# K scaled by GpSimd ahead of its transposes, and weight sums spread over two more phases, in a fused attention and gate kernel

## The chip, the cores and the metric

The kernel runs on one core of a Trainium2 chip. The metric is the device time of one execution, in microseconds (us). Every execution also has a mean granted TensorE clock: 1.0 is full speed, and TensorE runs at half speed for some microseconds after certain gaps. The mean is taken over the whole span, so half clock after the last matmul counts in it although it costs nothing.

## The reference, cut to what matters

Two branches read the same layer-normed `x` (2048 rows, 640 columns). One is attention with 32 heads of 192 columns over the last 512 rows of a key and value cache; the other is a gated feed-forward net (1536 hidden columns), whose output gates the first.

```python
q = (xn @ wq).reshape(B, Sq, 32, 192).transpose(0, 2, 1, 3)
scores = einsum("bhqd,bhkd->bhqk", q, k_last_512) * (192 ** -0.5)
s = (softmax(scores) @ v_last_512).transpose(...).reshape(B, Sq, 32 * 192) @ wo
h = sigmoid(xn @ w_gate) * (xn @ w_up)
g = silu(h @ w_down)
return x + s * g
```

## The kernel before

It first computes the gates (four stages of 512 rows, the last one ending at about 166 us) and stores them in device memory. Then it goes through 16 attention runs: 8 groups of 4 heads, each for two halves of the rows. Run r computes its scores (with the query projection of run r+1 between them) and then its weighted sums of V (with the output product of run r-1 between them). Only run 0 has its projection, "the first projection", by itself. In the views, `hT` is the hidden tile of the gate part, `gB` the finished gates, `qp` a copy of a projected query part and `qT` the finished query tile; a bank is a piece of the memory into which TensorE writes its results (`ps_all`), and HI is the second group of matmuls of the first projection, which needs VectorE's first query sum. Comments in the code cuts are mine, and `...` marks what is left out.

The query weights are scaled by a power of two (`w_up`), split into halves and added and subtracted in float16 (`scale_w` on ScalarE, `sum_w` on VectorE). Each group of heads has five such parts. The inverse of that scale is made up for in the Exp, which reads it from a one-column tile:

```python
def set_scale2(mx_row):
    ...
    nc.vector.tensor_scalar(w_down, mx, 1.0 / 4096, None, op0=ALU.mult)
    nc.vector.reciprocal(w_up, w_down)
    nc.vector.tensor_scalar(w_down, w_down, scale_qk, None, op0=ALU.mult)

def scale_w(g, c):                                   # ScalarE: 1.57 + 2 x 0.52 us
    raw = raw_t[g, c][:]
    nc.scalar.activation(raw.bitcast(F16), raw, AF.Copy, scale=w_up)
    for k, r in enumerate((LO, HI)):
        nc.scalar.activation(sums_w(g, c, r, 0), part_w(g, c, r, k, 0), AF.Copy)

def sum_w(g, c):                                     # VectorE: 4 x 0.36 us, ScalarE: 0.52 us
    ...
    tt(TB, part_w(g, c, a, 1, 1), part_w(g, c, a, 0, 1), ALU.subtract)     # two inputs in SBUF
    ...

def stage_s(r, i, pp, c, k):                         # scores: 6 matmuls and an Exp
    ...
    nc.scalar.activation(E_t[r, i, pp][:, c, :, :], ps, AF.Exp, scale=w_down)

def stage_pv(r, i, pp, h):                           # 16 matmuls, then VectorE
    if h == 0:
        ost_t[0] = (late["ost"] if r == last else ost_pool).tile(..., name="o_st")
    ...                                              # ost_pool has two buffers
    if h == 1:
        nc.sync.dma_start_transpose(oT[:], o_st[:]...)
```

The memory of the gate part is given to the pools of the attention part, in this order: `acc_pool`, `wo_pool`, `qT_pool`, `e_pool`, `ost_pool`, ... The first query tiles (`qT`) come to lie where the gate tiles (`gB_sb`) were, so whoever writes them waits for the last gate store.

The softmax here doesn't subtract the row's maximum and nothing guards it: scores larger than these inputs give would overflow.

Of the kernel before, what the change touches and what calls it, by code (L numbers as in the profile page):

```python
# [17 lines left out]
def kernel(  # L18
# [13 lines left out]
    nc = tc.nc  # L32
# [98 lines left out]
    def load_k(key):  # L131
# [6 lines left out]
            )  # L138
        k_of[key] = k_sb

    def turn_k(key):
        kT = kt_pool.tile([P, KC * PC, P], BF16, name="kT")
        nc.sync.dma_start_transpose(kT[:], k_of[key][:].rearrange("p n i e -> p (n i e)"))
        kT_t[key] = kT
# [43 lines left out]
    def set_scale2(mx_row):  # L188
        nc.vector.tensor_reduce(mx, mx_row[:], axis=mybir.AxisListType.X, op=ALU.max)
        nc.vector.tensor_scalar(mx, mx, 1e-30, None, op0=ALU.max)  # L190
        bits = mx.bitcast(I32)
        nc.vector.tensor_single_scalar(bits, bits, 0x7F800000, op=ALU.bitwise_and)
        nc.vector.tensor_scalar(w_down, mx, 1.0 / 4096, None, op0=ALU.mult)
        nc.vector.reciprocal(w_up, w_down)
        nc.vector.tensor_scalar(w_down, w_down, scale_qk, None, op0=ALU.mult)

    def load_raw(g, c, eng):
        raw = raw_pool.tile([P, 2, GC], BF16, name="raw")
# [31 lines left out]
    with ExitStack() as bctx:  # L230
# [185 lines left out]
        for s in range(NST):  # L416
# [4 lines left out]
            for f in range(NF):  # L421
# [26 lines left out]
                if s == 1 and f < NSB:  # L448
                    scan_load(NSB + f, nc.gpsimd)
                elif s == 2 and f < NPC - 2 * NSB:  # L450
                    scan_load(2 * NSB + f, nc.gpsimd)
                elif s == 2 and f < 5:
                    load_raw(0, f - 2, nc.gpsimd)
                elif s == 2 and f == 6:
                    set_scale(wmax, mx_row)
                elif s == 2 and f == NF - 1:
                    set_scale2(mx_row)
                elif s == 3:
                    if f == 0:
                        weight_tiles(0)  # L460
                    for c in {0: (0,), 2: (1,), 5: (2,), 7: (3,), 10: (4,)}.get(f, ()):
                        scale_w(0, c)
                    for c in {1: (0,), 3: (1,), 6: (2,), 8: (3,), 11: (4,)}.get(f, ()):
                        sum_w(0, c)
                        load_raw((c + 3) // NCD, (c + 3) % NCD, nc.gpsimd)
                    if f in (2, 6):
                        turn_k((0, f // 4))
                        load_k(divmod(f // 4 + 1, G))
            if s + 2 < NST:
                load_x4(s + 2)  # L470
            for q in range(TQ):
# [13 lines left out]
                    scan_fold(wmax, folds_q[s, q])  # L485
                if s == 3 and q in (1, 2):
                    sum_x(pi, 3 + q, sw)
                t = s * TQ + q
                nc.gpsimd.dma_start(gB_d[t * P:(t + 1) * P, :], gB_sb[:])
            if s == 0:  # L490
# [24 lines left out]
    wo_t = {}  # L515

    def load_wo(g):
        pool, eng = (late["wo"], nc.sync) if g == NG - 1 else (wo_pool, nc.scalar)
        wo_g = pool.tile([P, G * PC, D], BF16, name="wo_g")
        eng.dma_start(wo_g[:], wo_r[:, g * G * PC:(g + 1) * G * PC, :])  # L520
        wo_t[g] = wo_g
# [85 lines left out]
    def stage_s(r, i, pp, c, k):  # L607
        kT = kT_t[runs[r][1], pp]
        if c == 0:
            E_t[r, i, pp] = e_pool.tile([P, KC, 2, 512], BF16, name="E")  # L610
        b0 = 4 + 2 * (k % 2)
        ps = ps_all[:, b0:b0 + 2, :]
        for j in range(PC):
            for b, h in enumerate((LO, HI)):
                nc.tensor.matmul(  # L615
                    ps[:, b, :], lhsT=kT[h, c * PC + j, :], rhs=qT_t[r][i, j][h, pp, :],
                    start=(j == 0), stop=(j == PC - 1),
                )
        nc.scalar.activation(E_t[r, i, pp][:, c, :, :], ps, AF.Exp, scale=w_down)  # L619

    def stage_pv(r, i, pp, h):
        if h == 0:
# [67 lines left out]
    def stage_wo(r, i, q):  # L690
# [8 lines left out]
        oA = flat(bank2())  # L699
        wo_mm(oA, r, i, q, d_chunks)  # L700
        if g == NG - 1:
            finish(oA[:, 0:D], gates[t], t, 0, D, r == last and q % 2 == 1)
        elif g == 0:
            nc.vector.tensor_copy(acc[t][:], oA[:, 0:D])
        else:
# [3 lines left out]
    last = len(runs) - 1  # L709
    qT_t, E_t, oT_t, ost_t = {}, {}, {}, {}  # L710
    load_wo(0)
    slots = query_slots(0, True, (2, 3), (4, 5), (6, 7, 0))
    for n, k in enumerate((0, 1, 7, 2, 3, 8, 4, 5, 9, 6, 10)):
        slots[k]()
        if n in (1, 5):
            scale_w(1, n // 5)
        elif n in (3, 7):
            sum_w(1, n // 5)
            load_raw(1, n // 5 + 3, nc.gpsimd)
    sum_at = {2: (3,), 6: (4,)}, {0: (0,), 1: (1,), 3: (2,), 4: (3,), 6: (4,)}  # L720
    scale_at = {0: (3,), 2: (4,)}, {0: (2,), 3: (3,), 4: (4,)}
    q_after = {1: (0,), 2: (1,), 3: (2,), 4: (3,), 5: (4,), 6: (5, 6), 8: (7,), 10: (8,), 12: (9,), 14: (10,)}

    for r, (pi, g) in enumerate(runs):
# [3 lines left out]
        for k, x in enumerate(s_list):  # L728
# [1 line left out]
            for j in q_after.get(k, ()) if q_list else ():  # L730
                q_list[j]()
            if r == 0 and k == 6:
                scale_w(1, 2)
            elif r == 0 and k == 9:
                sum_w(1, 2)
            if r == last and k % 2 == 1:
                ring[:] = [0, 1]
                stage_wo(*wo_list[k // 2])
# [8 lines left out]
        if new_t is not None:  # L747
            if r > 0:
                weight_tiles(new_t)
                scale_w(new_t, 0)  # L750
                scale_w(new_t, 1)
        elif pi == 1 and g + 1 < NG:
            turn_k((g + 1, 0))
            load_k((g + 1, 1))
        if r == last - 1:
            qctx.close()
            for name, n in (("wo", 1), ("gate", 4 * TQ), ("fin", 2 * TQ), ("fout", 4), ("ost", 4), ("tmp", 2)):
# [21 lines left out]
                for c in scale_at[r > 0].get(k, ()):  # L779
                    scale_w(new_t, c)  # L780
        if new_t is not None and g + 2 < NG:
            for c in range(3):
                load_raw(g + 2, c, nc.gpsimd)
        if pi == 1 and g + 1 < NG:
            for pp in range(G):
# [37 lines left out]
```

## Time and profile before

The kernel before took 924.01 us (median of 3 runs, 923.84 to 927.41). Its profiled execution spans 925.7 us, and it was one of the slower ones (927.78 us, clock 0.994). I cut the trace at the first matmul of each stage:

| stage of the kernel before | start, us | length, us | TensorE busy, us |
|---|---|---|---|
| last products of the gates (from the first with `w_down`) | 151.96 | 14.51 | 13.40 |
| first projection | 166.47 | 18.71 | 14.21 |
| scores of run 0 (with the projection of run 1) | 185.18 | 24.38 | 22.98 |
| weighted sums of run 0 | 209.56 | 10.76 | |
| scores of run 1 | 220.32 | 28.31 | 25.14 |
| weighted sums of run 1, then runs 2 to 14 | 248.63 | | no gap |

Length less busy time is what waits cost in a stage. From 248 to about 868 us, where the scores of run 15 begin, TensorE counts as busy without a gap.

The columns of a timeline are start, duration, engine, line, operation, output and inputs, count of instructions in the group, and in brackets the idle time ahead of it and what ended it.

### The profile page before, as it was taken

The page shows a single profiled execution, that of the slowest core. Times are in us where ns is not written, and L with a number is a line of the kernel's source. Part 1 is how long each engine was busy: PE and PEld are TensorE (multiplying, and loading weights), DVE is VectorE, ACT ScalarE, POOL GpSimd, SP SyncE. Part 2 cuts the span into 40 slices and gives each one's busy share as a digit, 9 for nine tenths or more (in the row PEclk, how much of TensorE's full clock was granted, in tenths as well). Part 3 has the DMA queues.
Part 4 walks back from the last instruction along what each step waited for, and adds up shares of the span by engine and source line. Part 5 has one row for each costly group of instructions (what it writes and reads, how often), then busy time and mean ns, then how long its engine had stood idle before and what let it go on. Part 6 is the DMA issues. An engine that isn't in the chain of part 4 may idle for free. (4 is left out here: it accounts for less than half of the span.)

```text
span 925.7 us, 18472 instructions
## 1 busy us (share of the span) xinstructions
PE 905.0 (98%) x7785; PEld 537.4 (58%) x7785; DVE 650.8 (70%) x1091; ACT 466.3 (50%) x527; POOL 151.1 (16%) x184
## 2 busy tenths in 40 slices
PE   8999999898999999999999999999999999999997
PEld 5545454446565656565656565656666666666555
DVE  4879947566667866786678667866786678666556
ACT  4323346585618651855285528552854285434240
POOL 0052123101000200020002000200020000002961
PEclk9999999998999999999999999999999999999999
DMA  9993385216170837093708360826093615265625
GB/s 282 259 262 98 83 153 124 82 36 103 35 138 1 174 58 137 1 182 57 130 4 184 62 122 11 188 52 120 18 178 54 120 30 118 52 104 163 161 76 122
DMA packets 186610, 100.36 MB, mean 108 GB/s; under 512 B 153312, under 2 KB 178912, under 8 KB 186528
## 3 DMA queue, kind: packets, MB, share of 16 engines
q1 hardware_dynamic: 156848, 56.87, 31.2%
q0 software_dynamic: 9408, 29.93, 13.3%
q10 hardware_dynamic: 20272, 12.39, 5.7%
q8 instruction: 61, 1.00, 0.5%
q14 instruction: 21, 0.17, 0.1%
HBM read 57.87 MB, written 5.24 MB: 68 GB/s over the span
## 5 line engine op out<-in xcount | busy, mean ns | idle before, releaser
L619 ACT ACTIVATE E<-ps_all,w_sc 128x1024 bf16<-128x1024 f32 x256 | 275.3, 1114 | 280.0 <-PE ps_all L615 183.8
L672 PE MATMUL ps_all<-wo_g,oT 128*128 128x512 bf16 (+2 forms) x1536 | 228.4, 299 | 3.1 <-DVE o_sb L687 3.1
L615 PE MATMUL ps_all<-qT,kT 64*128 64x512 bf16 x1536 | 199.4, 378 | 2.3 <-ACT E L619 1.7
L629 PE MATMUL ps_all<-v_sb,E 128*128 128x193 bf16 x2048 | 189.5, 247 | 0.2 <-ACT E L619 0.2
L629 PEld LDWEIGHTS <-E 128*128 128x128 bf16 x2048 | 168.7, 98 | 18.2 <-issue 6.4
L672 PEld LDWEIGHTS <-oT 128*128 128x128 bf16 x1536 | 121.6, 98 | 82.6 <-issue 6.3
L563 DVE TENSOR_TENSOR qT<-ps_all,qp 128x512 bf16<-128x512 f32 x176 | 116.7, 687 | 53.8 <-PE ps_all L529 40.8
L550 DVE COPY qp<-ps_all 128x512 f32<-128x512 f32 x150 | 100.7, 688 | 63.3 <-PE ps_all L529 63.3
L615 PEld LDWEIGHTS <-kT 64*128 64x128 bf16 x1536 | 77.2, 94 | 93.4 <-issue 14.3
L636 DVE TENSOR_TENSOR o_st<-ps_all,rden 128x768 bf16<-128x768 f32 x128 | 122.5, 957 | 8.3 <-DMA oT<-o_st 4.0
L200 POOL DMA_DIRECT2D raw<-in_A_wq_dram x80 | 47.9, 603 | 323.9 <-ACT wB L225 234.1
L135 POOL DMA_DIRECT2D k_sb<-in_A_k_cache_dram x32 | 32.9, 1029 | 264.1 <-DMA kT<-k_sb 207.6
L216 ACT ACTIVATE raw<-raw,w_sc 128x1536 f16<-128x1536 bf16 x40 | 62.9, 1573 | 0.8
L529 PE MATMUL ps_all<-XA,wA 64*128 64x512 f16 x420 | 54.1, 385 | 2.5 <-ACT qp L548 2.0
L706 DVE TENSOR_TENSOR acc<-ps_all,acc 128x640 f32<-128x640 f32 x48 | 39.6, 824 | 21.9 <-PE ps_all L672 21.9
L475 PE MATMUL ps_all<-wd_sb,hT_sb 128*128 128x512 bf16 (+1 forms) x384 | 53.1, 299 | 1.1 <-DVE hT_sb L434 1.1
L529 PE MATMUL ps_all<-XB,wB 64*128 64x512 f16 x420 | 52.8, 376 | 0.5 <-ACT qp L548 0.5
L635 DVE RECIPROCAL rden<-ps_all 128x4 f32<-128x4 f32 x128 | 23.2, 181 | 42.5 <-PE ps_all L629 41.4
L529 PE MATMUL ps_all<-X,w 64*128 64x512 bf16 x420 | 51.9, 376 | 0.0
L434 DVE TENSOR_TENSOR hT_sb<-ps_all,sig_sb 128x512 bf16<-128x512 f32 x48 | 32.6, 683 | 25.5 <-ACT sig_sb L433 14.8
L433 ACT ACTIVATE sig_sb<-ps_all 128x512 bf16<-128x512 f32 x48 | 28.1, 596 | 40.2 <-PE ps_all L428 37.1
L706 DVE TENSOR_TENSOR acc_hi<-ps_all,acc_hi 128x640 f32<-128x640 f32 x48 | 39.3, 818 | 7.8 <-PE ps_all L672 7.8
(113 smaller groups left out, 730.0 us busy)
## 6 DMA issues: line engine op xcount, KB each, us to landing
raw<-in_A_wq_dram POOLq DMA_DIRECT2D x80, 192.0 KB, 3.9
wo_g<-in_A_wo_dram ACTq DMA_DIRECT2D x7, 960.0 KB, 6.8
k_sb<-in_A_k_cache_dram POOLq DMA_DIRECT2D x32, 192.0 KB, 4.6
v_sb<-in_A_v_cache_dram ACTq DMA_DIRECT2D x28, 192.0 KB, 3.9
gB_d<-gB_sb POOLq DMA_DIRECT2D x16, 160.0 KB, 3.1
gBa_sb<-gB_d SPq DMA_DIRECT2D x16, 160.0 KB, 3.8
xa_sb<-in_A_x_dram SPq DMA_DIRECT2D x16, 160.0 KB, 3.7
out_dram<-o_sb SPq DMA_DIRECT2D x15, 160.0 KB, 1.8
```

The costliest lines, as they stand in the source:

```text
L200: eng.dma_start(raw[r], wq_r[:, c, :, g * GC:(g + 1) * GC])
L216: nc.scalar.activation(raw.bitcast(F16), raw, AF.Copy, scale=w_up)
L475: nc.tensor.matmul(oB_ps[:, d0:d0 + dsz], lhsT=hT_sb[:, f, q * P:(q + 1) * P], rhs=wd_sb[:, f, d0:d0 + dsz], start=(f == 0), stop=(f == NF ...
L529: nc.tensor.matmul(ps_all[:, b, :], lhsT=w(r, c), rhs=x[r, c, :], start=(first and k == 0), stop=(k == len(cs) - 1), skip_group_check=True,)
L550: nc.vector.tensor_copy(dst, part(b))
L563: nc.vector.tensor_tensor(q_out(i, u, pp), part(b), t[:], ALU.add)
L615: nc.tensor.matmul(ps[:, b, :], lhsT=kT[h, c * PC + j, :], rhs=qT_t[r][i, j][h, pp, :], start=(j == 0), stop=(j == PC - 1),)
L619: nc.scalar.activation(E_t[r, i, pp][:, c, :, :], ps, AF.Exp, scale=w_down)
L629: nc.tensor.matmul(o_ps[:, q // 2, q % 2, 0:DH + 1], lhsT=E[:, c, h, q * P:(q + 1) * P], rhs=vt[:, c, 0:DH + 1], start=(c == 0), stop=(c = ...
L636: nc.vector.tensor_tensor(o_st[:, :, h * DH:(h + 1) * DH].rearrange("p (b i) d -> p b i d", b=2), o_ps[:, :, :, 0:DH], rden[:].to_broadcas ...
L672: nc.tensor.matmul(oA[:, d0 - base:d0 - base + dsz], lhsT=oT_t[r, i, pp][:, q * PC + j, :], rhs=wo_t[runs[r][1]][:, cc, d0:d0 + dsz], star ...
L706: nc.vector.tensor_tensor(acc[t][:], oA[:, 0:D], acc[t][:], ALU.add)
```

## The change

The intent is to take work off ScalarE and off the crowded start of the attention part. GpSimd multiplies each K tile by `w_down` in place, ahead of its transpose, so that the Exp's scale becomes a constant. Of the five scalings and sums of the second group, one less stands in the first projection; they are spread over run 0's scores, run 0's weighted sums and the first score step of run 1. The first output weights come over the sync queue, the Exp's table load is put ahead of the first projection, and at the very end one more row tile has its addition on GpSimd.

```diff
+    def scale_k(key):
+        nc.gpsimd.tensor_scalar(k_of[key][:], k_of[key][:], w_down, None, op0=ALU.mult)
 ...
-        nc.vector.tensor_scalar(w_down, w_down, scale_qk, None, op0=ALU.mult)
 ...
-                    if f in (2, 6):
-                        turn_k((0, f // 4))
-                        load_k(divmod(f // 4 + 1, G))
+                    if f in (0, 6):
+                        scale_k((0, f // 6))
+                    elif f in (3, 9):
+                        turn_k((0, f // 6))
+                    elif f == 5:
+                        load_k((0, 1))
 ...
+                elif s == 3 and q == 3:
+                    load_k((1, 0))                      # ahead of the last gate store
 ...
-        pool, eng = (late["wo"], nc.sync) if g == NG - 1 else (wo_pool, nc.scalar)
+        pool = late["wo"] if g == NG - 1 else wo_pool
+        eng = nc.scalar if 0 < g < NG - 1 else nc.sync
 ...
-        nc.scalar.activation(E_t[r, i, pp][:, c, :, :], ps, AF.Exp, scale=w_down)
+        nc.scalar.activation(E_t[r, i, pp][:, c, :, :], ps, AF.Exp, scale=scale_qk)
 ...
-            finish(oA[:, 0:D], gates[t], t, 0, D, r == last and q % 2 == 1)
+            finish(oA[:, 0:D], gates[t], t, 0, D, r == last and (q % 2 == 1 or (i, q) == (1, 2)))
 ...
     load_wo(0)
+    nc.scalar.activation(mx, w_up, AF.Exp, scale=0.0)   # table load
 ...
-        if n in (1, 5):                                 # first projection
-            scale_w(1, n // 5)
-        elif n in (3, 7):
-            sum_w(1, n // 5)
-            load_raw(1, n // 5 + 3, nc.gpsimd)
-    sum_at = {2: (3,), 6: (4,)}, {...}                  # run 0's weighted sums
-    scale_at = {0: (3,), 2: (4,)}, {...}
+        if n == 1:
+            scale_w(1, 0)
+        elif n == 3:
+            sum_w(1, 0)
+            load_raw(1, 3, nc.gpsimd)
+    sum_at = {2: (2,), 5: (3,)}, {...}
+    scale_at = {0: (2,), 1: (3,), 5: (4,)}, {...}
 ...
             if r == 0 and k == 6:
-                scale_w(1, 2)
+                scale_w(1, 1)
             elif r == 0 and k == 9:
-                sum_w(1, 2)
+                sum_w(1, 1)
+                load_raw(1, 4, nc.gpsimd)
+            elif r == 1 and k == 0:
+                sum_w(1, 4)
+                load_raw(2, 2, nc.gpsimd)
 ...
+            scale_k((g + 1, 0))
             turn_k((g + 1, 0))
             load_k((g + 1, 1))
+            scale_k((g + 1, 1))
 ...
-            for c in range(3):
+            for c in range(3 if r > 0 else 2):
                 load_raw(g + 2, c, nc.gpsimd)
```

More of the change, by code (lines that the diff above doesn't have):

```diff
@@ L714 @@
         slots[k]()
-        if n in (1, 5):
-            scale_w(1, n // 5)
-        elif n in (3, 7):
-            sum_w(1, n // 5)
-            load_raw(1, n // 5 + 3, nc.gpsimd)
-    sum_at = {2: (3,), 6: (4,)}, {0: (0,), 1: (1,), 3: (2,), 4: (3,), 6: (4,)}
-    scale_at = {0: (3,), 2: (4,)}, {0: (2,), 3: (3,), 4: (4,)}
+        if n == 1:
[3 more added lines that the diff above has]
+            load_raw(1, 3, nc.gpsimd)
+    sum_at = {2: (2,), 5: (3,)}, {0: (0,), 1: (1,), 3: (2,), 4: (3,), 6: (4,)}
+    scale_at = {0: (2,), 1: (3,), 5: (4,)}, {0: (2,), 3: (3,), 4: (4,)}
     q_after = {1: (0,), 2: (1,), 3: (2,), 4: (3,), 5: (4,), 6: (5, 6), 8: (7,), 10: (8,), 12: (9,), 14: (10,)}
```

## The prediction

> **What bounds the kernel now.** I read the page's busy times first, then stretches by stage, then the list of waits, then the timeline where the stretches show a gap.
>
> ```profile
> PE 905.0 (98%) x7785; PEld 537.4 (58%) x7785; DVE 650.8 (70%) x1091; ACT 466.3 (50%) x527; POOL 151.1 (16%) x184
> ...
> L619 ACT ACTIVATE E<-ps_all,w_sc 128x1024 bf16<-128x1024 f32 x256 | 275.3, 1114 | 280.0 <-PE ps_all L615 183.8
> ```
>
> TensorE is busy 905.0 of 925.7 us. The Exp row, the costliest group, has more idle time before it (280.0) than work (275.3), ended by TensorE: ScalarE mostly waits for TensorE. The stretches show where the remainder lies (start:end, length, then PE, PEld, DVE, ACT, POOL busy, the granted clock, DMA share, GB/s):
>
> ```profile
> 166.00:185.00 19.00, 14.51 (x108) 7.03 (x107) 9.47 (x19) 12.85 (x20) 1.83 (x4) 0.91 0.29 90
> 185.00:209.50 24.50, 23.14 (x206) 11.47 (x203) 16.67 (x29) 21.65 (x24) 2.31 (x4) 1.00 0.13 34
> ...
> 220.30:248.60 28.30, 25.14 (x203) 11.73 (x201) 17.74 (x30) 16.86 (x17) 1.55 (x3) 0.88 0.38 69
> 248.60:271.00 22.40, 22.40 (x217) 17.30 (x216) 14.52 (x23) 1.26 (x2) 3.76 (x4) 1.00 0.67 119
> 868.00:897.00 29.00, 25.89 (x199) 11.90 (x198) 12.42 (x15) 16.96 (x16) 26.32 (x20) 1.00 0.52 145
> ```
>
> From 248.6 to about 868 TensorE is busy without a gap at full clock, in every stretch I asked for: there only fewer matmuls would help, and the change removes none. What can be won is in 166 to 249, the first query projection and the first two attention runs. How much: the third run's scores plus projection take 272.45 to 294.47, 22.0 us, undisturbed; ten projection matmuls follow each other at 1.08 us. So the first projection (110 matmuls) needs 11.9 us and takes 18.7 (166.47 to 185.18): 6.8 lost. Run 0 takes 24.4 (185.18 to 209.56): 2.4 lost. Run 1 takes 28.3 (220.32 to 248.63): 6.3 lost. **Some 15.5 us is the pool**, 1.7% of the span. The timeline says why:
>
> ```profile
> 168.44 0.54 POOL L489 DMA_DIRECT2D gB_d<-gB_sb  x1 [2.72 <-DVE gB_sb L483]
> ...
> 170.80 0.44 ACTq L520 DMA_DIRECT2D wo_g<-in_A_wo_dram  x1
> 171.29 1.08 ACT L548 ACTIVATE qp<-ps_all 128x512 f32<-128x512 f32 x2 [4.00 <-DMA gB_d<-gB_sb]
> 171.94 0.37 PE L529 MATMUL ps_all<-XA,wA 64*128 64x512 f16 x1 [2.05 <-ACT qp L548]
> ...
> 172.72 5.08 PE L529 MATMUL ps_all<-XA,wA 64*128 64x512 f16 x29 [0.41 <-DVE qT L563]
> ...
> 222.90 0.96 DVE L636 TENSOR_TENSOR o_st<-ps_all,rden 128x768 bf16<-128x768 f32 x1 [1.96 <-DMA oT<-o_st]
> 223.77 0.35 DVE L223 TENSOR_TENSOR acc_hi<-raw 128x384 f16<-128x384 f16 x1
> 223.91 1.30 PE L529 MATMUL ps_all<-X,acc_hi 64*128 64x512 bf16 x10 [2.12 <-DVE o_st L636]
> ```
>
> **Stall A** (170 to 173): the output weights' load stands on ScalarE's queue and waits for the last gate store, because it is put into memory that the gates used; ScalarE's copies stand behind it. **Stall B** (180 to 187): copies, two rounds of weight scaling and an Exp table load share ScalarE. **Stall C** (221 to 226): VectorE's `o_st` waits for the transpose of an earlier `o_st` (two buffers), TensorE waits for the bank that it frees. A and C are followed by lower clock (0.50 in the 2 us slices at 174 and at 226 to 230).
>
> **What the Trainium skill says.** *ScalarE: Activation LUTs*, section What ACT_TABLE_LOAD costs: a table load is about 1283 ns, and each [128,1] pointer operand of an ACTIVATE adds about 93 ns. The trace has 1283 ns for the load; the Exp takes 1114 ns with its scale read from a tile, so I estimate 1021 ns with the constant. *GPSIMD Engine Reference*, section Performance versus the Vector engine: bodies of at most two operations per element run at 1.03 cycles per element at 1.2 GHz. An estimate for 128x1536 is 1.3 us plus dispatch, say 1.5 us; this trace has only two-input GpSimd work (1.40 us for 640 columns). *SBUF — State Buffer*, section Who interferes with whom: a VectorE instruction with two SBUF inputs and a GpSimd instruction that reads SBUF exclude each other. The trace of before doesn't show it. *TensorE: Matmul & The Clock Gate*, Part 1: the clock halves after an idle window of some 3.4 us that runs freely. The trace agrees in kind: half clock after both long gaps.
>
> **The change part by part.**
> 1. Exp with a constant: 256 x 93 ns = 23.8 us off ScalarE. On the path only where ScalarE is the limit, that is run 0: sixteen Exps, 1.5 us, of which I count 0.5 us.
> 2. K scaled on GpSimd: 16 x 1.5 us = 24 us on an engine at 16%, almost all hidden. The K transposes now wait for it. In steady runs the second K tile of a group is loaded by about 253 (issued 248.24, 4.6 us to landing) and transposed after the fourth weighted sum, about 260: 7 us of slack for 1.5. In the gated part the second scaling falls near 147 to 150, beside two-input VectorE sums whose results gate the last `hT`; TensorE already waits there (1.1 us at 156). I charge 0.3 us.
> 3. Output weights on the sync queue: ScalarE's first copy waits no more. But the built program's list of waits shows that VectorE's first query sum still waits for all four gate stores, the last included, since its tile too lies in their memory; TensorE's HI matmul needs that sum. So the stall shortens only to landing + sum: before, landing about 170.75 and HI start 172.72. The next K load is also moved ahead of the last gate store on the same queue (2.1 us of issue, starting at about 165.7); I estimate the store lands 0.3 us later, 171.05; sum 0.7; HI at about 171.85. Won: 0.9 us.
> 4. First projection with one scaling round fewer (1.57 + 1.05 + 0.52 = 3.1 us off ScalarE) and the table load moved ahead of it, into ScalarE's wait. Walking the copies, sums and groups of matmuls in their new order with their old durations from HI at 171.85: slots end near 182.0 at full clock, against 185.2 to 185.5. That is 3.5 us, the 0.9 of part 3 in it. With half clock for one window after stall A it ends near 184: 1.5 us won. I take 2.8.
> 5. Run 1: sum 4 moves from behind the seventh `o_st` into run 1, so the eighth bank comes 1.5 us earlier. The first wait remains: the seventh `o_st` hangs on the second transpose (issued 217.6, landed 222.9), and nothing in the change makes that earlier. ScalarE now does two scalings, then waits for sum 3 at about 12 us into the weighted sums, then scales chunk 4, so its first Exp of run 1 comes some 15.3 us in, where before it came 15.5 us in (225.09). Won: about 0.4 us.
> 6. End: the last but one tile's addition goes to GpSimd, VectorE is free 0.8 us earlier; the sync queue issues that tile's store (GpSimd done about 921.7) ahead of the last two halves. Won: 0.3 us.
>
> Sum: 0.5 + 2.8 + 0.4 + 0.3 - 0.3 = 3.7 us, so 920.3. The clock after a gap is partly chance: the before runs spread from 923.84 to 927.41. With a shorter stall A the drop may be absent more often (half a window is 1.7 us); I move the middle to 919.5.
>
> **Rivals.** (a) *The wait only changes its name*: the K load before the last gate store delays it by 1 us or more, stall A stays as long, TensorE gets half clock again. For it: same queue, 2.1 us of issue. Against: the K load at 248.24 moved its data within about 4 us. The time would be 922 to 924. (b) *Both gaps fall below what halves the clock*, and run 1's sums come free early: the whole lost clock (1.7 us and some 3.4 us) comes back too. For it: 46% busy around stall A was enough for a drop, and 180 to 187 at about 65% was not. Against: stall C's cause is a transpose. Time 914 to 916. (c) *GpSimd becomes the limit* through in-order waits: a scaling stuck behind loads that wait for weight buffers delays a K transpose until TensorE waits. Against: 16% busy, 7 us of slack. Time 930 or more. (d) *Nothing*, because fewer scalings only move to runs 0 and 1, which then lose what the projection won: about 924.
>
> **Range and chances.** (a) and (d) give the upper part, (b) the lower; eight in ten between 914.5 and 923.5. Faster by over 2% needs 905.5 or less, 18.5 us, more than the pool of 15.5; slower by over 2% needs a new steady wait. So 0.01 and 0.01, within 2% 0.98.
>
> **What would show it.** Right: Exp near 1021 ns; VectorE's first query sum, no longer ScalarE, ending the first TensorE gap at about 171.9; projection ending at 181 to 184; the gap before run 1's first projection still ended by `o_st`, with half clock after it; GpSimd scaling 1.3 to 2.4 us each and no TensorE gap at a K transpose; all from 250 to 868 unchanged. Wrong: a gap in the steady part, GpSimd scalings of several us, or run 1 without its gap, which would mean that the transpose was late for a reason I missed.

## More of the kernel before

One more view, needed later, is the timeline at the end of the score stage of run 2.

The answers for ScalarE and for TensorE:

```profile
290.26 5.44 ACT L619 ACTIVATE E<-ps_all,w_sc 128x1024 bf16<-128x1024 f32 x5
```

```profile
291.67 1.60 PE L615 MATMUL ps_all<-qT,kT 64*128 64x512 bf16 x12
...
294.47 1.51 PE L629 MATMUL ps_all<-v_sb,E 128*128 128x193 bf16 x16
```

ScalarE runs the last five Exps of the stage without a pause, at 1.09 us each, while TensorE shows no gap either: both sides look full.

## The result, and the profile after

The changed kernel took 920.70 us (median of 4 runs, 919.98 to 921.61), and on the same chip the kernel before took 924.69 us (median of 4, 923.84 to 927.41). The ratio is 0.9952, 95% interval 0.9929 to 0.9976. Ratios here are the mean time of one kernel's fast runs over the mean of the other's fast runs of the same rounds, so not quite the ratio of the medians. All outputs agreed with the reference, here and in every run below.

The page of the changed kernel: the engines' busy times, the Exp row, and the row that is new.

```profile
PE 896.2 (97%) x7706; PEld 533.6 (58%) x7785; DVE 653.5 (71%) x1089; ACT 446.1 (49%) x528; POOL 220.3 (24%) x201
...
L627 ACT ACTIVATE E<-ps_all 128x1024 bf16<-128x1024 f32 x256 | 253.3, 1022 | 295.4 <-PE ps_all L623 224.3
...
L142 POOL TENSOR_SCALAR k_sb<-k_sb,w_sc 128x1536 bf16<-128x1536 bf16 x16 | 67.1, 4193 | 22.2 <-DMA k_sb<-in_A_k_cache_dram 21.9
```

The Exp takes 1022 ns, as predicted. A K scaling takes 4193 ns, not 1.5 us. (79 matmul records are missing from this trace, 7706 of 7785, so its TensorE busy time can't be compared with the 905.0 us of before.)

The stretches of the changed kernel (length, then TensorE, weight load, VectorE, ScalarE, GpSimd busy, granted clock, DMA share, GB/s): end of the gates, first projection, scores of run 0, scores of run 1.

```profile
151.70:169.00 17.30, 14.86 (x97) 7.83 (x99) 10.91 (x15) 7.39 (x11) 5.04 (x9) 0.90 0.39 94
169.00:183.50 14.50, 12.04 (x106) 5.56 (x107) 8.02 (x15) 11.08 (x18) 3.08 (x5) 1.00 0.51 138
183.50:207.50 24.00, 22.73 (x204) 11.30 (x200) 16.46 (x28) 19.41 (x23) 1.19 (x2) 1.00 0.07 18
218.30:243.30 25.00, 22.40 (x202) 11.43 (x201) 19.13 (x34) 18.76 (x21) 6.54 (x5) 1.00 0.51 92
```

Against the kernel before the lost clock has moved: the first projection and run 1 are now at 1.00 (0.91 and 0.88 before), and the end of the gates is at 0.90 (1.00 before). The projection's own time fell from 18.71 to 14.59 us; but it starts at 168.96 instead of 166.47.

The timeline of the changed kernel just ahead of the projection says why it starts late:

```profile
147.20 4.67 POOL L142 TENSOR_SCALAR k_sb<-k_sb,w_sc 128x1536 bf16<-128x1536 bf16 x1
...
149.69 1.53 DVE L225 TENSOR_TENSOR wB<-raw 128x384 f16<-128x384 f16 x1
...
151.64 0.52 ACT L227 ACTIVATE wB<-raw 64x384 f16<-64x384 f16 x1 [2.59 <-DVE wA L226]
...
155.81 0.45 PE L480 MATMUL ps_all<-wd_sb,hT_sb 128*128 128x512 bf16 x2 [1.23 <-DVE hT_sb L436]
```

The same place in the kernel before, where GpSimd only issues a K load (147.21, 2.07 us):

```profile
149.82 0.35 DVE L223 TENSOR_TENSOR wB<-raw 128x384 f16<-128x384 f16 x1
...
150.60 0.52 ACT L225 ACTIVATE wB<-raw 64x384 f16<-64x384 f16 x1 [1.41 <-DVE wA L224]
...
156.32 1.48 PE L475 MATMUL ps_all<-wd_sb,hT_sb 128*128 128x512 bf16 x9 [1.10 <-DVE hT_sb L434]
```

While GpSimd scales, VectorE's two-input sum takes 1.53 us instead of 0.35. ScalarE's copy that needs the sum comes about a microsecond later, and with it everything behind it in ScalarE's queue, the last sigmoids included; TensorE waits for the last `hT` twice, 1.23 us and then, at 157.35, 1.10 us, where before it waited only once, for 1.10 us. In this profile half clock follows at 156 to 162. In this profile three VectorE sums were held by a scaling (at 131.48, 149.69 and 759.03 us, for 0.1 to 1.9 us), and each ended about 0.65 us before the recorded end of that scaling. It works the other way too: the scaling shown began while VectorE was in a sum of two inputs (146.38 to 147.85 us) and took 4.67 us, where the other fifteen took 4.15 to 4.18.

Stalls A and C of the prediction, in the changed kernel:

```profile
169.78 1.28 ACT L720 ACT_TABLE_LOAD   x1
...
170.91 0.57 POOL L496 DMA_DIRECT2D gB_d<-gB_sb  x1 [0.62 <-DVE gB_sb L488]
...
171.19 1.06 ACT L556 ACTIVATE qp<-ps_all 128x512 f32<-128x512 f32 x2
...
173.86 1.29 DVE L571 TENSOR_TENSOR qT<-ps_all,qp 128x512 bf16<-128x512 f32 x2 [3.24 <-ACT raw L218]
174.61 0.61 PE L537 MATMUL ps_all<-XA,wA 64*128 64x512 f16 x4 [2.03 <-DVE qT L571]
```

```profile
220.69 0.96 DVE L644 TENSOR_TENSOR o_st<-ps_all,rden 128x768 bf16<-128x768 f32 x1 [0.23 <-DMA oT<-o_st]
...
221.70 1.45 PE L537 MATMUL ps_all<-X,acc_hi 64*128 64x512 bf16 x10 [1.94 <-DVE o_st L644]
```

The first copy is done at 171.8, but VectorE's sum starts at 173.86. The profile names ScalarE's weight scaling (L218, done at 173.71) as its releaser, but the sum does not read what that writes. What it waited for is the landing of the last gate store, as the prediction had it: the trace has that at 173.64, and in all nine profiles with this wait (after, e1, e2, e3, e5, e6, e8, e11, e12) TensorE's second group starts 0.96 or 0.97 us after the store has landed. In run 1 the gap ended by `o_st` is still there (1.94 us, 2.12 before), but no half clock follows it.

**Counting the clock.** I looked for half clock in slices of 2 us over the whole attention part of every profile, up to its last matmul, and added up (1 - clock) x 2 us. The sum always came out as 0, 1.7, 3.4 or 5.1 us. So half clock comes in units, each costing about 1.7 us. The Trainium skill, *TensorE: Matmul & The Clock Gate*, Part 1, speaks of a window of 3413 ns that runs freely; one window at half speed loses 1.707 us, and every profile agrees. The kernel before had three units in its profile (one in the projection, two in run 1), the changed kernel one.

The traces also show what the chance in it is. A stretch at half clock lasts 3.41 us (6.83 us once, in run 1 of the kernel before), and within a profile the starts lie whole multiples of 3.413 us apart (173.79 and 224.99 us in the kernel before: 15 times). So each profile has a fixed grid of windows, and where a gap falls in it differs from run to run. I continued the grid through all 14 profiles, from about 7 us to the last matmul, and counted TensorE's busy time in each window (matmul ends are modelled, so the limit is rough). Half clock followed all 12 windows with at most 1.467 us busy of the 3.41. It followed 4 of the 11 windows with 1.471 to 1.746 us, and no fuller one, but for the second unit in run 1 of the kernel before, which follows a window at half clock. So a gap of 2 us that lies inside one window is near the limit, and one that is spread over two windows is not. At run 1's first gap the window has 1.30 us busy in the kernel before (221.58 to 224.99 us, half clock after it) and 1.471 us in the changed kernel (218.35 to 221.77 us, none after it).

| | before | after | difference |
|---|---|---|---|
| start of the last gate products | 151.96 | 151.69 | -0.3 |
| last gate products | 14.51 | 17.27 | +2.8 |
| first projection | 18.71 | 14.59 | -4.1 |
| scores of run 0 | 24.38 | 23.98 | -0.4 |
| scores of run 1 | 28.31 | 25.04 | -3.3 |
| from run 1's weighted sums to those of run 15 | 648.2 | 647.6 | -0.6 |
| from run 15's weighted sums to the end | 28.9 | 28.8 | -0.1 |
| span | 925.7 | 919.7 | -6.0 |
| units of half clock in it | 3 | 1 | -3.4 us |

Of the 6.0 us between the two profiles, up to 3.4 are clock. In the times, which mix runs of all clocks, the difference of the medians is 4.0 us.

### The profile page after: what moved, and what is told of

It reads as the page before. It is cut to its first block, busy times and chain, and to the rows that moved or that the text cites. A ratio compares the mean times of both kernels' runs of the same rounds, so it can differ in the third digit from the quotient of the medians.

```text
span 919.7 us, 18431 instructions
## 1 busy us (share of the span) xinstructions
PE 896.2 (97%) x7706; PEld 533.6 (58%) x7785; DVE 653.5 (71%) x1089; ACT 446.1 (49%) x528; POOL 220.3 (24%) x201
## 4 chain that ended last, share of the span: by engine, by line
PE 87%; DVE 4%; ACT 4%; DMA 3%; issue 2%; POOL 0%; SPq 0%; DVEq 0%; POOLq 0%; ACTq 0%
PE ps_all L680 21%; PE ps_all L537 19%; PE ps_all L637 17%; PE ps_all L623 16%; PE ps_all L430 8%; PE ps_all L480 4%; ACT raw L218 1%; ACT E L627 1%; DVE ps_all L694 1%; DVE o_sb L695 1%; PE ps_all L344 1%; ACT sig_sb L435 1%; DMA gB_d<-gB_sb 1%; DVE wB L225 1%; DMA oT<-o_st 1%
## 5 line engine op out<-in xcount | busy, mean ns | idle before, releaser
L627 ACT ACTIVATE E<-ps_all 128x1024 bf16<-128x1024 f32 x256 | 253.3, 1022 | 295.4 <-PE ps_all L623 224.3
L680 PE MATMUL ps_all<-wo_g,oT 128*128 128x128 bf16 (+2 forms) x1474 | 225.1, 296 | 6.4 <-DVE o_sb L695 3.1
L623 PE MATMUL ps_all<-qT,kT 64*128 64x512 bf16 x1536 | 195.3, 376 | 1.9 <-ACT E L627 1.0
L142 POOL TENSOR_SCALAR k_sb<-k_sb,w_sc 128x1536 bf16<-128x1536 bf16 x16 | 67.1, 4193 | 22.2 <-DMA k_sb<-in_A_k_cache_dram 21.9
L218 ACT ACTIVATE raw<-raw,w_sc 128x1536 f16<-128x1536 bf16 x40 | 63.0, 1575 | 1.1
L480 PE MATMUL ps_all<-wd_sb,hT_sb 128*128 128x128 bf16 (+1 forms) x377 | 54.2, 303 | 2.7 <-DVE hT_sb L436 2.3
L436 DVE TENSOR_TENSOR hT_sb<-ps_all,sig_sb 128x512 bf16<-128x512 f32 x48 | 32.6, 683 | 25.5 <-ACT sig_sb L435 14.8
```

What stands on the lines that cost most here:

```text
L142: nc.gpsimd.tensor_scalar(k_of[key][:], k_of[key][:], w_down, None, op0=ALU.mult)
L480: nc.tensor.matmul(oB_ps[:, d0:d0 + dsz], lhsT=hT_sb[:, f, q * P:(q + 1) * P], rhs=wd_sb[:, f, d0:d0 + dsz], start=(f == 0), stop=(f == NF ...
L623: nc.tensor.matmul(ps[:, b, :], lhsT=kT[h, c * PC + j, :], rhs=qT_t[r][i, j][h, pp, :], start=(j == 0), stop=(j == PC - 1),)
L680: nc.tensor.matmul(oA[:, d0 - base:d0 - base + dsz], lhsT=oT_t[r, i, pp][:, q * PC + j, :], rhs=wo_t[runs[r][1]][:, cc, d0:d0 + dsz], star ...
```

## The experiments

Twelve kernels, each an edit of the changed one. A chip's kernel before had medians of 923.6 us (first four kernels), 925.9 (the next four), 925.25 (the next three) and 925.26 (the last), so the ratios are to be compared, not the microseconds. "Half clock" is the sum over the profile up to the last matmul; "span less half clock" takes it off whole, which is a little too much where TensorE would have waited anyway.

| kernel | median us | ratio to before, 95% | profile: span | half clock | span less half clock | projection starts | projection | run 0 | run 1 |
|---|---|---|---|---|---|---|---|---|---|
| before | 924.69 | 1 | 925.7 | 5.1 | 920.6 | 166.47 | 18.71 | 24.38 | 28.31 |
| after | 920.70 | 0.9952 (0.9929 to 0.9976) | 919.7 | 1.7 | 918.0 | 168.96 | 14.59 | 23.98 | 25.04 |
| e1 | 920.14 | 0.9949 (0.9931 to 0.9967) | 918.8 | 1.7 | 917.1 | 166.56 | 16.19 | 23.98 | 24.91 |
| e2 | 921.05 | 0.9968 (0.9949 to 0.9987) | 918.9 | 0 | 918.9 | 166.76 | 14.52 | 24.38 | 24.92 |
| e3 | 925.39 | 1.0014 (0.9995 to 1.0033) | 923.2 | 3.4 | 919.8 | 168.96 | 16.28 | 23.98 | 26.78 |
| e4 | 925.18 | 1.0008 (0.9990 to 1.0026) | 922.7 | 1.7 | 921.0 | 167.61 | 18.72 | 23.99 | 24.93 |
| e5 | 921.27 | 0.9955 (0.9932 to 0.9977) | 918.8 | 0 | 918.8 | 168.09 | 14.58 | 23.98 | 25.01 |
| e7 | 921.38 | 0.9948 (0.9931 to 0.9966) | 921.1 | 3.4 | 917.7 | 169.75 | 13.49 | 23.98 | 26.39 |
| e8 | 921.52 | 0.9954 (0.9933 to 0.9975) | 918.8 | 1.7 | 917.1 | 168.13 | 14.58 | 23.98 | 25.90 |
| e9 | 917.87 | 0.9910 (0.9891 to 0.9928) | 917.1 | 1.7 | 915.4 | 166.58 | 13.50 | 23.98 | 26.55 |
| e11 | 923.88 | 0.9975 (0.9952 to 0.9999) | 922.2 | 3.4 | 918.8 | 167.49 | 16.31 | 23.97 | 27.31 |
| e12 | 921.72 | 0.9957 (0.9937 to 0.9978) | 920.6 | 3.4 | 917.2 | 169.30 | 16.21 | 23.98 | 23.96 |
| e10 | 915.76 | 0.9894 (0.9874 to 0.9915) | 913.8 | 0 | 913.8 | 165.94 | 13.49 | 23.98 | 23.96 |
| e6 | 920.51 | 0.9944 (0.9909 to 0.9979) | 918.6 | 1.7 | 916.9 | 167.29 | 13.94 | 23.98 | 26.22 |

**e1: the first group's K scaled by VectorE.** Is it GpSimd's scaling that makes the projection start late?

```diff
-        nc.gpsimd.tensor_scalar(k_of[key][:], k_of[key][:], w_down, None, op0=ALU.mult)
+        eng = nc.vector if key[0] == 0 else nc.gpsimd
+        eng.tensor_scalar(k_of[key][:], k_of[key][:], w_down, None, op0=ALU.mult)
 ...
-                    if f in (0, 6):
-                        scale_k((0, f // 6))
+                    if f in (1, 8):
+                        scale_k((0, f // 8))
```

> The changed kernel with the first group's two K tiles scaled by VectorE in place of GpSimd (one phase step later, when the tile has landed). Theory C (the 4.2 us GpSimd scaling collides with a two-input VectorE sum, delays the last hT and costs about 2.5 us before the first projection): the first projection starts near 166.5 us instead of 169.0, no half clock at 157 to 161, time about 918. Rival S (the gap at 154 to 158 comes of ScalarE's weight scaling alone and would be as long without GpSimd): projection still starts near 169, time about 920.7.

It is. The timeline of e1 at the same place:

```profile
149.90 0.35 DVE L226 TENSOR_TENSOR wB<-raw 128x384 f16<-128x384 f16 x1
...
151.46 0.62 DVE L143 TENSOR_SCALAR k_sb<-k_sb,w_sc 128x1536 bf16<-128x1536 bf16 x1
...
156.40 1.80 PE L481 MATMUL ps_all<-wd_sb,hT_sb 128*128 128x512 bf16 x12 [0.98 <-DVE hT_sb L437]
```

The sum takes 0.35 us again, VectorE's scaling takes 0.62 us where GpSimd's took 4.67, and the projection starts at 166.56, 2.4 us earlier. But the time gained less than the start did: in this profile half clock came up in stall A (172 to 178), and the projection took 16.19 us.

**e2: no K scaling.** The Exp reads its scale from a tile again, everything else stays.

```diff
-        nc.gpsimd.tensor_scalar(k_of[key][:], k_of[key][:], w_down, None, op0=ALU.mult)
+        pass
 ...
         nc.vector.reciprocal(w_up, w_down)
+        nc.vector.tensor_scalar(w_down, w_down, scale_qk, None, op0=ALU.mult)
 ...
-AF.Exp, scale=scale_qk)
+AF.Exp, scale=w_down)
```

> The changed kernel with the K scaling undone: no GpSimd scaling, Exp reads its scale from the tile again. Theory C: the gap at 154 to 158 shrinks to that of the kernel before (2.5 us back), the longer Exp (1114 against 1022 ns) costs 0.5 us in run 0, so about 918.5: the K scaling is a net loss. Rival E (the shorter Exp is what made the gain): about 924 or more.

The start of the projection came back (166.76), run 0 is 24.38 us as before, and yet the time is no better. The rest is in the long part that I had called unchanged: its score stages take 22.02 us in the kernel before and in e2, and 21.90 us in every kernel with the constant scale. Twelve such stages give 1.4 us. The end of the score stage of run 2 in the changed kernel, ScalarE and TensorE, against the lines of the kernel before above:

```profile
284.84 1.94 ACT L627 ACTIVATE E<-ps_all 128x1024 bf16<-128x1024 f32 x2
287.22 2.96 ACT L627 ACTIVATE E<-ps_all 128x1024 bf16<-128x1024 f32 x3 [0.44 <-PE ps_all L623]
```

```profile
286.36 1.46 PE L623 MATMUL ps_all<-qT,kT 64*128 64x512 bf16 x12
```

Before, five Exps ran without a pause and ScalarE set the pace, and the wait lay inside TensorE's last groups (1.60 us for 12 matmuls, now 1.46). With the shorter Exp, ScalarE has to wait for TensorE again (0.44 us).

**e3: the weight sums where they were.** The second group's scalings and sums stand as in the kernel before, the other parts of the change stay (the edit undoes the hunks of `scale_w`, `sum_w`, `sum_at`, `scale_at` and the range of `load_raw`).

> The changed kernel with the second group's weight scalings and sums placed as in the kernel before (two in the first projection, one in run 0, two in run 0's weighted sums). Theory P (3.1 us less of ScalarE in the first projection is most of the 4.1 us that it got shorter): projection about 3 us longer, time about 923 to 924. Rival T (the early table load and the freed queue are most of it): projection at most 1 us longer, about 921.

This part is worth most. The projection is 16.28 us against 14.59, both at full clock in their profiles: 1.7 us, between the two readings of the expectation; the time is worse than either. Run 1 is 1.74 us longer, but that is one unit of half clock (224 to 230 us), so it alone does not show what the sums do to run 1.

**e4: the first output weights on ScalarE's queue again.**

```diff
-        eng = nc.scalar if 0 < g < NG - 1 else nc.sync
+        eng = nc.scalar if g < NG - 1 else nc.sync
```

> The changed kernel with the first output weights issued from ScalarE's queue again. Theory P: VectorE's first query sum waits for the last gate store in any case, so ScalarE's copies and the first scaling start about 2 us later but TensorE's HI matmul only about 1 us later; time plus 0.5 to 1.5 us, about 921.7. Rival Q (the queue was the gain): plus 3 us or more, about 924.

Worse than predicted for this part, and nearer to the rival. The trace shows why: the other line of the change that came with it, the table load, stands behind the output weights.

```profile
172.53 0.44 ACTq L528 DMA_DIRECT2D wo_g<-in_A_wo_dram  x1
173.00 1.28 ACT L720 ACT_TABLE_LOAD   x1 [4.59 <-DMA gB_d<-gB_sb]
...
175.04 0.37 PE L537 MATMUL ps_all<-XA,wA 64*128 64x512 f16 x1 [4.02 <-ACT qp L556]
```

ScalarE waits 4.59 us for the gate store, then loads the table, then copies; TensorE's gap is 4.02 us, where the kernel before, with the weights on the same queue but the table load later, has 2.05 and 0.41 us. The two parts belong together.

**e5: the table load back ahead of the first Exp.**

```diff
-    nc.scalar.activation(mx, w_up, AF.Exp, scale=0.0)
```

> The changed kernel without its early Exp table load, so that the load comes just ahead of the first Exp again. Theory P (the prediction's part 4: ahead of the projection the load lies in a wait of ScalarE and costs nothing, ahead of the first Exp it stands on the path): run 0 of attention gets 0.5 to 1.3 us longer, about 24.8 instead of 24.0 us; time 921.3 to 922.2 against 920.7 for the changed kernel. Rival H (ScalarE has room there too, or the first copies of the projection gain what the first Exp loses): time 920.5 to 921.0, run 0 unchanged within 0.2 us.

The rival was right: projection 14.58 and run 0 23.98 us, the same as with it. The load then falls at 183.48, the first Exp comes 2.1 us after the start of the scores instead of 0.9, and that is made up within the stage. The early table load is worth nothing here.

**e6: the K load behind the last gate store on GpSimd's queue.**

```diff
-                elif s == 3 and q == 3:
-                    load_k((1, 0))
                 t = s * TQ + q
                 nc.gpsimd.dma_start(gB_d[t * P:(t + 1) * P, :], gB_sb[:])
+                if s == 3 and q == 3:
+                    load_k((1, 0))
```

> The changed kernel with the K load of the second group behind the last gate store on GpSimd's queue, not ahead of it. Theory P (the prediction's part 3 charged this order 0.3 us, for 2.1 us of issue that lie in GpSimd's wait for the last gate product): the second group of projection matmuls starts at 5.35 to 5.65 us from the start of the projection, in place of 5.65; ratio 0.994 to 0.9955. Rival a (the load ahead of it delays the store by 1 us or more): it starts at 4.7 us or earlier, the gap of 2.03 falls below 1.2 us, ratio 0.9935 to 0.9945.

In between: the second group of projection matmuls starts 4.99 us after the first instead of 5.65, and the gap is 1.37 us instead of 2.03. From the end of the store's issue to VectorE's sum it is 1.75 us (169.79 to 171.54) where it was 2.38 (171.48 to 173.86). So the K load ahead of it costs 0.6 to 0.7 us, twice what the prediction charged; the time shows none of it, within its interval.

**e7: the first query tiles in other memory.** The pool of the Exp results is laid out first, so the query tiles no longer lie where the gate tiles were. Nothing else is touched, and no wait is taken out by hand.

```diff
+    e_pool = ctx.enter_context(tc.tile_pool(name="e_pool", bufs=2 * G))
     wo_pool = ctx.enter_context(tc.tile_pool(name="wo_pool", bufs=1))
     qT_pool = ctx.enter_context(tc.tile_pool(name="qT_pool", bufs=10))
-    e_pool = ctx.enter_context(tc.tile_pool(name="e_pool", bufs=2 * G))
```

> The changed kernel with the pool of the Exp results laid out ahead of the output weights and the query tiles, so that the first query tiles no longer lie where the gate tiles were; nothing else is touched. Theory P (the prediction's part 3: VectorE's first query sum waits for the last gate store only because of where its tile lies): the gap of 2.03 us ahead of the second group of projection matmuls vanishes or falls below 0.5 us, the first projection takes 12.3 to 13.3 us instead of 14.6, time 918.5 to 919.5. Rival T (the copy, the sum and the table load themselves take that long): the gap stays at 1.5 us or more, ended by a copy or a sum of the same start, time 920.3 to 921.0.

```profile
172.59 1.29 DVE L571 TENSOR_TENSOR qT<-ps_all,qp 128x512 bf16<-128x512 f32 x2 [1.18 <-ACT qp L556]
...
176.26 1.04 PE L537 MATMUL ps_all<-XA,wA 64*128 64x512 f16 x8 [0.62 <-ACT qp L556]
```

The sum now waits for the copy alone: it starts at 172.59, while the last gate store lands only at 177.43. The gap of 2.03 us is gone, and one of 0.62 us has come up one slot later, behind ScalarE's weight scaling. The projection takes 13.49 us: 1.1 us won, less than the 1.3 to 2.3 expected. The median hides it: this profile has two units of half clock elsewhere, ahead of the projection and in run 1.

**e8: the last group's first K scaling earlier.** The changed kernel's score stage at 770 us (run 13) takes 22.74 us, where all its neighbours take 21.90. Its timeline:

```profile
757.78 4.17 POOL L142 TENSOR_SCALAR k_sb<-k_sb,w_sc 128x1536 bf16<-128x1536 bf16 x1
...
759.03 2.27 DVE L225 TENSOR_TENSOR wB<-raw 128x384 f16<-128x384 f16 x1
...
772.30 1.04 PE L537 MATMUL ps_all<-X,w 64*128 64x512 bf16 x8 [0.66 <-DVE o_st L644]
```

It is the same collision. In the earlier groups weight loads stand ahead of the scaling in GpSimd's queue; the last group has none left to load, so the scaling starts early, beside VectorE's sums.

```diff
-            scale_k((g + 1, 0))
+            if g + 2 < NG:
+                scale_k((g + 1, 0))
             turn_k((g + 1, 0))
 ...
                     load_k((g + 2, 0))
+                    if g + 3 == NG:
+                        scale_k((g + 2, 0))
```

> The changed kernel with the first scaling of the last head group's K issued just behind its load, three quarters through the weighted sums of run 11, and not two stages later. Theory C (the late loss of the changed kernel, a score stage of 22.74 instead of 21.90 us at 770 us and 0.15 us ahead of it, is that scaling, running beside VectorE's weight sums at 757 to 762): that stage comes back to 21.9 us, time 0.7 to 1.0 us less, 919.7 to 920.0. Rival O (the loss is something else of the last groups, such as their loads): that stage stays at 22.7, time 920.4 to 921.0.

The stage is back at 21.90 us, and the weighted sums ahead of it at 23.82 (23.95 in the changed kernel), so the cause is shown. The 0.85 us do not show in the median; in this profile run 1 has a unit of half clock that the changed kernel's profile lacks.

**e9: e1, e7 and e8 together.**

> Three edits of the changed kernel together: the first group's K scaled by VectorE, the pool of the Exp results laid out first, the last group's first K scaling early. Theory S (three separate losses: about 2.4 us ahead of the projection, 1.5 to 2 in stall A, 0.85 at 770): projection starts at 166.6 and takes about 12.5 us, no half clock is left before 250 us, time 915.5 to 916.5. Rival K (the half clock comes up somewhere else when the earlier one goes, as when K alone went to VectorE): projection 14 us or longer or half clock in run 0, time 917 to 918.5.

The projection starts at 166.58 and takes 13.50 us, as the three alone say, and half clock comes up in run 1 (218 to 224). The ratio is 0.9910. The two readings of the expectation each have part of it: three separate losses as in theory S, but half clock elsewhere and a time (917.87 us) as in rival K.

**e11: only the last of the five sums put back, ahead of the eighth `o_st` of run 0.**

```diff
-    sum_at = {2: (2,), 5: (3,)}, {...}
+    sum_at = {2: (2,), 5: (3,), 6: (4,)}, {...}
 ...
-            elif r == 1 and k == 0:
-                sum_w(1, 4)
-                load_raw(2, 2, nc.gpsimd)
 ...
-            for c in range(3 if r > 0 else 2):
+            for c in range(3):
```

> The changed kernel with one move of the weight sums undone: the last one of the second group stands again behind the seventh o_st of run 0, ahead of the eighth, and not in run 1. Theory P (the prediction's part 5: it holds the eighth bank 1.5 us longer): TensorE's first gap in run 1 is about as before (1.9 to 2.1 us, ended by the seventh o_st), a second one of about 1.5 us comes behind it, run 1 takes 26.0 to 26.8 us without half clock and about 28 with it, time 1.2 to 3 us over the changed kernel: ratio to the kernel before 0.996 to 0.9985 where the changed kernel has 0.9952. Rival N (the sum has room where it was; what run 1 won is only the clock of one profiled run): run 1 as the changed kernel's in the same state of the clock, ratio 0.9945 to 0.996.

Run 1 took 27.31 us with one unit of half clock in it, so 25.6 without: some 0.5 us more than the changed kernel's 25.04. The second gap that theory P asked for is 1.07 us and is ended by an Exp, not 1.5 us and by `o_st`. The kernel before and e3, with the sum in the same place, have 1.04 and 1.00 us there; the kernels with the sum moved have 0.52 to 0.75 (none in e8). So the sum's place is worth about 0.4 us in that gap. The ratio rises from 0.9952 to 0.9975, but those two intervals overlap, and its runs have lower clocks (0.993 to 0.997) than the changed kernel's (0.997 to 0.999). Whether the place of the sum makes half clock more frequent, I can't settle: the kernel before has the sum there too, and 5 of its 11 runs beside e1 to e4 had a clock of 0.999 or 1.000.

**e12: a third place for `o_st` in run 0**, in a part of the accumulators that is unused by then, so that the seventh `o_st` does not wait for the second transpose.

```diff
-            ost_t[0] = (late["ost"] if r == last else ost_pool).tile(..., name="o_st")
+            ost_t[0] = None if r == 0 and (i, pp) == (1, 0) else (late["ost"] if r == last else ost_pool).tile(..., name="o_st")
+            if r == 0 and (i, pp) == (1, 0):
+                ost_t[0] = hi_flat[:, 4 * n_w:4 * n_w + 2 * TQ * DH // 2].bitcast(BF16).rearrange(...)
```

> The changed kernel with a third place for o_st in run 0 (the third of its four lies in the unused end of the accumulators), so that the seventh o_st no longer waits for the second transpose. Theory P (stall C hangs on the transpose alone): VectorE's waits for a transpose at 215 and 220 us vanish, TensorE's gap ahead of run 1's first projection matmul falls from 1.94 to below 0.8 us, run 1 takes 23.0 to 24.2 us in place of 25.04, no half clock after it, time 919.0 to 920.0 on a chip where the kernel before has 923.6 to 924.7, ratio 0.993 to 0.9945. Rival N (the bank comes free late because VectorE's sums and o_st fill the time anyway): the gap stays above 1.2 us, ratio 0.9945 to 0.996.

```profile
221.36 0.96 DVE L646 TENSOR_TENSOR o_st<-ps_all,rden 128x768 bf16<-128x768 f32 x1
...
222.37 1.65 PE L537 MATMUL ps_all<-X,acc_hi 64*128 64x512 bf16 x10 [0.66 <-DVE o_st L646]
```

VectorE's two waits for a transpose (1.12 and 0.23 us in the changed kernel) are gone, TensorE's gap is 0.66 us instead of 1.94, and run 1 takes 23.96 us. Stall C is settled. The time shows nothing of it, because this profile, and by their clocks half of these runs, have two units of half clock in the other two stalls.

**e10: all four, e1, e7, e8 and e12.** A first build of a third buffer as a pool of three did not fit in memory; it ran to no chip.

> The four edits of the changed kernel together: first group's K scaled by VectorE, pool of the Exp results first, last group's first K scaling early, third place for o_st in run 0. Theory S (losses are separate, and with both long gaps gone the half clock goes too): as the kernel with three of them, which has a ratio of 0.991 to the kernel before, less 1.0 to 2.5 us: ratio 0.9885 to 0.990, clock 1.0 in nearly all runs, run 1 takes 23.0 to 24.2 us. Rival K (half clock comes up elsewhere): ratio 0.990 to 0.9915.

915.76 us (5 runs, 915.63 to 916.27), ratio 0.9894: 1.1% faster than the kernel before, with an interval that lies below that of the changed kernel. All five runs lie within 0.7 us, where the kernel before spreads over 4.7 us in the same rounds. In its profile no half clock comes up while TensorE works: the only stretch begins at 911.0 us, and the last matmul ended at 908.7. With the long gaps of all three stalls gone, the half clock is gone too.

## Why the prediction was right or wrong

The time was right (919.5 predicted, 920.70 measured, in the range), but it came out of several wrong terms that cancel, so that it lies this close is in part luck. Two of the signs that the prediction itself set for being wrong came: GpSimd scalings of several us (4.2), and a gap in the steady part (0.66 us at 772.30). Measured terms are from the table of the two profiles.

1. **Exp with a constant: size right, reach wrong.** 1022 ns measured, 1021 estimated; run 0 won 0.4 us (0.5 predicted). "All from 250 to 868 unchanged" was wrong: each steady score stage fell from 22.02 to 21.90 us, 1.4 us over twelve stages. The step that failed is the reading of "busy without a gap at full clock" as "there only fewer matmuls would help". The wait was inside the pipelined matmuls' busy time, and ScalarE's five Exps in a row showed it. Run 13 gave 0.9 of that back through the collision that e8 removes.
2. **K on GpSimd: the term that was mis-sized.** "128x1536 is 1.3 us plus dispatch, say 1.5 us" came from the rate that it cites; the scaling took 4.2 us. So it did not fit beside the sums, and the charge of 0.3 us became 2.8 us in the profile. By e1 it is all GpSimd's scaling. Without half clock the last gate products took 15.8 to 16.5 us in e4, e5, e6, e8 and e11, and 14.5 to 14.8 in the kernel before, e1, e2, e9 and e10: 1.0 to 2.0 us of waiting. A unit of half clock came on top in four of nine profiles with the scaling on GpSimd (after, e3, e7, e12), never in the five without. The mechanism (the exclusion) had been named; its length had not. In the steady runs the 7 us of slack held, so rival (c) did not come, but the last group's scaling ran into the sums, which the prediction had not looked for.
3. **Output weights on the sync queue: mechanism right.** VectorE's first sum, waiting for the last gate store, ended stall A; the second group of matmuls started 5.65 us into the projection, 6.25 before, so 0.6 us won and 0.9 predicted. The K load ahead of the store costs 0.6 to 0.7 us (e6), not 0.3: rival (a) was half right. That the tile's place causes the wait is shown by e7.
4. **First projection: too small.** 2.8 us predicted, 4.1 measured, with no half clock in this profile; 1.7 of the 4.1 is the unit that the kernel before has there. With half clock it is 16.19, 16.31 and 16.21 us (e1, e11, e12), a gain of 2.4 to 2.5, where the prediction's two cases were 3.5 and 1.5. One round of scaling fewer is 1.7 us of it (e3). The table load, counted as a help, is worth nothing (e5), and is a harm with the weights on ScalarE's queue (e4).
5. **Run 1: 0.4 us predicted, 3.3 in the profile.** The gap stayed, ended by `o_st`, as predicted; "with half clock after it" did not come. Two units of half clock in the profile of before (3.4 us) are the whole difference. Without them run 1 is 24.9 to 25.1 us in the kernel before and in the changed one; e11 gives the moved sum some 0.4 us. With the sums moved, the same gap is followed by half clock in e6, e7, e8 and e9 (gaps of 1.88 to 2.08 us) and not in the changed kernel, e1, e2, e4 and e5 (1.60 to 2.04 us). So most of this is luck of one profile (where the gap fell in the grid of windows), not a part of the gain.
6. **End: 0.3 predicted, about 0.1 measured.** VectorE is done earlier, but the last but one tile now comes out of two GpSimd additions in a row (3.16 us, to 915.81). The sync queue issues that tile's store at 915.84 and only then the last two, at 916.27 and 916.77, though VectorE was done at 916.08. No experiment took this part alone.

Rival (b), that the lost clock comes back, is what the pair of profiles seems to show; over all runs it is only partly so. The changed kernel's four runs have clocks of 0.997 to 0.999, and 919.98 us is its fastest, with 0.999. The before's fastest on that chip is 923.84. So about 3.9 of the 4.0 us are there with good clocks too, by one run of each kernel, close to the predicted sum of 3.7 without its allowance for the clock. The two profiles less their half clock give 2.6 us (920.6 and 918.0), so the gain without the clock is known only as 2.6 to 3.9 us.

What stays open: why the clock of e3 and e11 is lower in nearly all runs than that of the changed kernel, with gaps of nearly the same length. Each has one profile, which does not show where the gaps of the other runs fell in their windows.

## What to carry to other kernels

An operation moved to an idle engine must be timed there first, and checked for what it excludes while it runs: a scaling of 4.2 us on an engine that was busy 16% of the time cost up to 2.8 us, because VectorE's sums stood still beside it. "TensorE busy without a gap" is no proof that TensorE sets the pace: look for a row of instructions without a pause on the engine that feeds it. Where gaps of about 2 us decide whether the clock drops, look how much of each window of 3.41 us they leave busy, compare profiles with the half clock taken off, and shorten every such gap rather than one of them: here each gap alone was lost in the clock of the others, and all three together, below 1 us each, gave 1.1%.

## What the Trainium skill lacked or had wrong

- *GPSIMD Engine Reference*, section Performance versus the Vector engine: the rate of 1.03 cycles per element for bodies of at most two operations does not hold for this one-input instruction. 128x1536 in bfloat16 with the scale from a tile took 4149 ns at least, which at the page's 1.2 GHz is an estimated 3.2 cycles per element. VectorE took 0.62 us for the same (e1).
- *SBUF — State Buffer*, section Who interferes with whom: the exclusion of a two-input VectorE instruction and a GpSimd instruction that reads SBUF is confirmed (0.35 us became 1.53 and 2.27 us). What the page lacks is that the held sums ended some 0.65 us before the recorded end of the GpSimd instruction, and the effect: a held sum carried ScalarE's queue and then TensorE with it, 1.0 to 2.0 us and sometimes a unit of half clock.
- *TensorE: Matmul & The Clock Gate*, section Why this matters for your kernels, asks for no idle gaps over about 3 us. Here a gap of 1.6 to 2.2 us, and two gaps of 1.23 to 1.80 and 1.10 us close together, were followed by half clock in about half of the profiles. With gaps of 0.61 to 0.66 us in their place no profile showed it there (e7, e9, e10 in stall A; e10, e12 in run 1).
- The same page, Part 1, lets the clock fall after at least one idle window. Here the window ahead of half clock was not idle: TensorE counts as busy for 0.37 to 1.75 us of the 3.41. The stretches of 3.41 us (1.71 us lost in each) fit the page's window of 3413 ns; one kernel's profile has up to three units, 5.1 us.
